# Attention with two kinds of heads and a gated feed-forward: the second chunk's keys and queries come as casting loads of a pair of heads in the software queue

## The chip, the cores and the metric

The kernel runs on one core of a Trainium2 chip. The metric is the device time of one execution in microseconds; the time of the kernel before is a median of three runs. "PE" in profile rows is TensorE, "PEld" its weight loads, "DVE" VectorE, "ACT" ScalarE, "POOL" GpSimd, "SP" SyncE. The "software queue" holds the DMAs that POOL issues (it can cast while loading), the "hardware queue" those that SP and ACT issue.

## What is computed

Four batches, eight heads, 768 positions, head size 64. Three heads see all earlier positions, five see a window of 64 and the first four positions. The attention output, 3072 tokens of 512, goes through a feed-forward of width 2048 with a gated activation.

```python
scores = scale * np.matmul(q, k.transpose(0, 1, 3, 2))       # q, k, v: (4, 8, 768, 64) f32
causal = rel >= 0
stream_keep = causal & (is_sink | in_win)                    # 4 sinks, window 64
a = np.exp(np.where(mask, scores, -1e9) - max)
out = np.matmul(a / a.sum(), v)                              # -> x: (3072, 512)
h = x @ w_in                                                 # (512, 2048)
g = h * (1.0 / (1.0 + np.exp(-beta * h)))
return g @ w_out                                             # (2048, 512)
```

## The kernel before

The work is cut into eight chunks of 384 tokens (three tiles of 128), two per batch. For each chunk the kernel brings keys and queries with the head dimension on partitions (two heads, a "pair", fill 128), makes scores in transposed form, exponentiates them on ScalarE, multiplies masks on VectorE, sums weighted values on TensorE (`products`, L882), scales (`x`, L906), transposes the result (`x_transposed`, L909), then runs the first product with `w_in` (L939, sixteen blocks of four matmuls), tanh on ScalarE (L941), the gate on VectorE (L943), the second product with `w_out` (L958), and stores 128 rows at a time. All data is computed in bf16 and summed in f32.

Every step is a `Task` with a planned duration; `Plan.run` (L128) plays the plan and so fixes, at build time, the order in which each engine's instructions stand. TensorE's next task is the one with the lowest key of `pe_key` (L1013): its place in the feed-forward (`STEPS`), moved by `LEAD`, `LEADS` and by a table `NUDGE` of single corrections. At run time each engine goes through its list in order and only waits on semaphores. Where TensorE would idle in the first 36 us by the plan, `fill` (L1036) puts matmuls on zeros.

The first two chunks start the kernel and get their own way of loading, from chunk three on rows are cast by the software queue and transposed by DMA on SP.

Chunks one and two (`F32_KQ`, L362, is true for chunk 0 and, by `F32_1 = "kq"`, for chunk 1): `load_pair` (L555) loads a pair's keys or queries as f32 from the hardware queue, 192 KB, one DMA; `keys_ramp` (L633) casts them to bf16 (`cast`, on VectorE or ScalarE, L458 by the helper `copy`), transposes them with three full 128 x 128 matmuls against the identity (L654), and copies the result from PSUM into `KT` or `QT` (L458). The token order inside a pair is p-major ("(p t) d"), so that each partition reads 768 bytes in one piece; the copy puts the columns back in order with a stride.

The software queue carries, in the order of `SW_ORDER` (L357), the values of chunk 0 (`v0`, three DMAs of 128 KB written), a hold (`h1`, a one-element POOL copy that waits for the first chunk's last key load and lets the second chunk's fourth pair start), the four column blocks of `w_in` (`i0` to `i3`, 512 KB each), the values of chunk 1 (`v1`) and the four row blocks of `w_out` (`o0` to `o3`). Not more than eight DMAs of this queue are in flight: an issue waits for the landing of the one eight places earlier.

`load_heads` (L602) and the branch of `keys_rows` (L662) for `KQ_PE` chunks are in the code but not used before the change.

```python
F32_1 = "kq"                                                       # L350
SW_ORDER = "v0 h1 i0 i1 v1 i2 o0 i3 o1 o3 o2".split()              # L357
casts[name] = P.add(f"cast{name}{c}.{p}", [dve(n, 0.53), act(n, 20)], [LD[name, c, p]], ...)   # L644
```

Of the kernel before, what the change touches and what calls it, by code (L numbers as in the profile page):

```python
# [9 lines left out]
BF16 = mybir.dt.bfloat16  # L10
# [68 lines left out]
class Plan:  # L79
# [10 lines left out]
    BEFORE, BEHIND, MARGIN, EARLY, LATER, FIRST = 1000.0, 1000.0, 100.0, 8900.0, 1000.0, 900.0  # L90
# [17 lines left out]
    def next_landing(self):  # L108

        now, left = self.moved, {q: [x[:] for x in l] for q, l in self.queues.items()}  # L110
        while True:
# [7 lines left out]
            turn = sum(left[q][0][2].land[2] for q in live)  # L119
# [120 lines left out]
    [(3, 3), (3, 2), (3, 3), (2, 2), (3, 3), (1, 1), (2, 2), (3, 3), (2, 2)],  # L240
    [(4, 3), (4, 3), (4, 0), (3, 0), (4, 3), (2, 3), (8, 8), (4, 4), (3, 3), (3, 3), (3, 3)],
    [(11, 10), (11, 11)],
    [(12, 12), (12, 11), (10, 10), (8, 0)],
    [(11, 10), (11, 11)],
    [(12, 12), (12, 12), (9, 7), (9, 2)],
    [(11, 10), (11, 11)],
    [(12, 12), (12, 12), (7, 7), (11, 2)],
]
F2_LAG = 12.0
RAMP = 40000.0  # L250
NUDGE = {
# [93 lines left out]
}  # L345
PARTS = [(3, 3)] * 4
LAST = 1
F32_1 = "kq"
MASK_C = 1
LEAD = 0.95  # L350
LEADS = {2: 1.6, 6: 0.9, 3: 0.9, 5: 0.9, 7: 1.0}
STORE_LATE = 1000.0
TURN = 33.0
X_PE = 3
PACE = {3: (2,), 5: (2, 8), 6: (3, 2), 7: (4, 0)}
FILL_END, FILL_SPARE = 36000.0, 120.0
# [18 lines left out]
def kernel(  # L375
# [13 lines left out]
    nc = tc.nc  # L389
# [709 lines left out]
```

## Time and profile before

| | |
|---|---|
| median of three runs | 225.69 us (224.97, 225.69, 227.6) |
| the profiled execution's own time | 225.52 us |
| its span, first to last instruction | 223.4 us, granted TensorE clock 0.998 |
| TensorE busy | 213.5 us (96%) |
| VectorE, ScalarE, POOL busy | 155.5, 144.5, 84.2 us |
| read from memory, written to it | 27.27 MB, 6.29 MB |
| first matmul of the first product, of the second chunk's | 22.12 us, 42.38 us |

The page of the profile has busy time by engine, then the span in 40 slices of 5.6 us with each engine's busy tenths, the DMA queues, the chain of waits that ended last, and the costliest groups of instructions. A timeline row gives start and length in us, engine, line, operation, output<-input tiles, and in brackets how long the engine sat idle ahead of it and what ended that. A matmul's row is longer than the time to the next one, since matmuls are pipelined; the time from start to start is what it costs.

### The profile page before, as it was taken

What the parts mean: (1) busy time and instruction counts of PE and PEld (TensorE: products, weight loads), DVE (VectorE), ACT (ScalarE), POOL (GpSimd) and SP (SyncE); (2) the same over time, 40 slices, a digit from 0 to 9 for tenths busy, and PEclk for the clock granted to TensorE, in tenths of its full rate; (3) what the DMA queues carried; (4) which work ended last, traced back from release to release, by engine and by line L of the source; (5) the groups of instructions that cost most, each with busy time, mean ns of one, the idle gap of its engine ahead of it and who ended that gap; (6) DMA issues with size and microseconds to landing.
All of it is one profiled execution on the core that took longest, in us unless ns stands there. A gap on an engine that the chain in (4) does not pass through costs nothing.

```text
span 223.4 us, 5079 instructions
## 1 busy us (share of the span) xinstructions
PE 213.5 (96%) x1842; PEld 123.7 (55%) x1866; DVE 155.5 (70%) x445; ACT 144.5 (65%) x292; POOL 84.2 (38%) x125
## 2 busy tenths in 40 slices
PE   7978999999999999999999999999999999999993
PEld 3546556554565555655554566455564655555552
DVE  5979995487687697779766777578765874437341
ACT  4887984484856798278756978069837793268310
POOL 7931533746995929800990397000000000000000
PEclk9999999999999999999999999999999999999999
DMA  6999999999999999998999499930104130011022
GB/s 197 247 238 197 201 206 199 123 149 144 167 151 135 210 160 179 142 130 226 86 136 166 128 143 154 137 111 22 47 18 102 47 85 2 0 50 47 1 94 94
DMA packets 102568, 28.32 MB, mean 127 GB/s; under 512 B 90880, under 2 KB 99600, under 8 KB 102544
## 3 DMA queue, kind: packets, MB, share of 16 engines
q0 software_dynamic: 67200, 12.07, 75.4%
q1 hardware_dynamic: 34480, 15.41, 33.2%
q10 hardware_dynamic: 864, 0.53, 0.8%
q8 instruction: 14, 0.23, 0.4%
q14 instruction: 10, 0.08, 0.1%
HBM read 27.27 MB, written 6.29 MB: 150 GB/s over the span
## 4 chain that ended last, share of the span: by engine, by line
PE 80%; DMA 10%; ACT 3%; DVE 3%; issue 2%; SPq 1%; ACTq 0%
PE bank L958 34%; PE bank L939 34%; PE bank L898 6%; PE bank L844 5%; DMA ks<-in_k_dram 5%; DMA xT<-x 2%; DMA qs<-in_q_dram 2%; SPq L560 1%; ACT th L941 1%; DVE gT L943 1%; ACT es L862 1%; PE bank L920 1%; DMA out_dram<-osb 1%; DVE VO L458 1%; DVE osb L971 0%
## 5 line engine op out<-in xcount | busy, mean ns | idle before, releaser
L941 ACT ACTIVATE th<-bank,beta_h 128x384 f32<-128x384 f32 x128 | 73.3, 590 | 36.6 <-PE bank L939 29.4
L939 PE MATMUL bank<-xT,w_in_sb 128*128 128x384 bf16 x512 | 90.5, 326 | 0.3 <-DMA xT<-x 0.2
L958 PE MATMUL bank<-w_out_sb,gT 128*128 128x512 bf16 (+1 forms) x376 | 87.7, 370 | 1.8 <-issue 0.6
L943 DVE SCALAR_TENSOR_TENSOR gT<-th,bank 128x384 bf16<-128x384 f32 x128 | 68.7, 550 | 26.4 <-ACT th L941 21.7
L862 ACT ACTIVATE es<-bank 128x512 bf16<-128x512 f32 (+3 forms) x137 | 62.8, 561 | 22.0 <-PE bank L844 18.0
L939 PEld LDWEIGHTS <-w_in_sb 128*128 128x128 bf16 x512 | 48.5, 98 | 34.0 <-issue 0.8
L958 PEld LDWEIGHTS <-gT 128*128 128x128 bf16 x400 | 37.5, 98 | 37.0 <-issue 0.5
L598 POOL DMA_DIRECT2D ks<-in_k_dram x36 | 26.9, 785 | 8.7 <-DMA w_out_sb<-in_moe_w_out_dram 3.1
L598 POOL DMA_DIRECT2D qs<-in_q_dram x36 | 26.9, 789 | 6.4 <-DMA w_out_sb<-in_moe_w_out_dram 3.6
L870 DVE TENSOR_TENSOR es<-es,M 128x384 bf16<-128x384 bf16 (+3 forms) x73 | 23.0, 333 | 6.7 <-ACT es L862 6.0
L570 POOL DMA_DIRECT2D VX<-in_v_dram x24 | 21.7, 946 | 0.0
L898 PEld LDWEIGHTS <-es 128*128 128x128 bf16 x472 | 17.2, 97 | 6.2 <-issue 2.3
L971 DVE TENSOR_SCALAR osb<-bank 128x512 f32<-128x512 f32 (+1 forms) x18 | 11.6, 646 | 11.7 <-PE bank L958 11.5
L844 PE MATMUL bank<-QT,KT 64*128 64x128 bf16 (+2 forms) x275 | 19.8, 242 | 0.0
L898 PE MATMUL bank<-VX,es 128*128 128x65 bf16 x392 | 17.9, 193 | 0.6 <-DVE x L906 0.6
L844 PEld LDWEIGHTS <-KT 64*128 64x128 bf16 x275 | 12.3, 94 | 9.9 <-issue 8.5
L906 DVE TENSOR_TENSOR x<-bank,rec 128x384 bf16<-128x384 f32 x32 | 17.0, 548 | 0.3
L870 DVE TENSOR_TENSOR es<-es,Mc 128x128 bf16<-128x128 bf16 (+1 forms) x42 | 9.9, 249 | 5.8 <-ACT es L862 5.5
L458 DVE COPY VO<-VX 128x512 bf16<-128x512 bf16 (+3 forms) x20 | 9.2, 475 | 2.1 <-DMA VX<-in_v_dram 2.0
L844 PE MATMUL bank<-QT,KO 64*128 64x128 bf16 x75 | 10.2, 217 | 0.0
L898 PE MATMUL bank<-VO,es 128*128 128x65 bf16 x80 | 9.1, 193 | 1.1 <-DVE VO L458 1.1
L969 ACT ACTIVATE osb<-bank 128x512 f32<-128x512 f32 (+1 forms) x9 | 4.7, 526 | 8.3 <-DVE osb L971 4.9
(58 smaller groups left out, 84.6 us busy)
## 6 DMA issues: line engine op xcount, KB each, us to landing
out_dram<-osb SPq DMA_DIRECT2D x23, 256.0 KB, 2.4
VX<-in_v_dram POOLq DMA_DIRECT2D x24, 128.0 KB, 6.9
ks<-in_k_dram POOLq DMA_DIRECT2D x36, 64.0 KB, 4.3
qs<-in_q_dram POOLq DMA_DIRECT2D x36, 64.0 KB, 4.4
w_in_sb<-in_moe_w_in_dram POOLq DMA_DIRECT2D x4, 512.0 KB, 15.9
w_out_sb<-in_moe_w_out_dram POOLq DMA_DIRECT2D x4, 512.0 KB, 16.1
ks<-in_k_dram SPq DMA_DIRECT2D x8, 192.0 KB, 4.7
qs<-in_q_dram SPq DMA_DIRECT2D x6, 192.0 KB, 6.4
```

Source lines behind the costliest of these rows:

```text
L570: LD["v", c, t] = dma(f"ldv{c}.{t}", "POOL", 800, 880, TURN, deps, lambda e, t=t, r=r: e.dma_start(out=VH[c].buf[:, t, :, 0:D], in_=v[b, : ...
L598: ROW[name, c, t] = [dma(f"row{name}{c}.{t}.{a}", "POOL", 750, 440, TURN, list(deps), lambda e, t=t, a=a, r=r, i=i, src=src: e.dma_start(o ...
L844: nc.tensor.matmul(bank.buf[:, at * 128:(at + n) * 128], x["k"](), QH[c].buf[half(a), x["p"], x["q"] * 128:(x["q"] + n) * 128], start=not ...
L862: te = P.add(f"exp{c}.{s}", [act(w * 128)], [t], c * 100 + first_p * 10, lambda _, w=w, bank=bank, es=es: nc.scalar.activation(out=es.buf[ ...
L870: nc.vector.tensor_mul(e, e, other)
L898: nc.tensor.matmul(view()[:, i, a, 0:D + 1], e.buf[:, at * 128:(at + 1) * 128], val(), start=(j == 0), stop=(j == len(lst) - 1))
L906: nc.vector.tensor_mul(xo, view()[:, :, :, 0:D], rec.buf[:, 0:nt].to_broadcast([128, nt, 2, D]))
L939: nc.tensor.matmul(bank.buf[:, 0:n], w_in_sb[:, mo, fi * 128:(fi + 1) * 128], XTH[c].buf[:, mo, 0:n], start=(mo == 0), stop=(mo == MO - 1))
L941: t = P.add(f"th{c}.{fi}", [act(n, 97)], [t, t_beta], c * 100, lambda _, fi=fi, bank=bank, th=th: nc.scalar.activation(out=th.buf[:, 0:n], ...
L943: GATE[c, fi] = P.add(f"gate{c}.{fi}", [dve(n)], [t], c * 100, lambda _, fi=fi, bank=bank, th=th: nc.vector.scalar_tensor_tensor(out=GH[c] ...
L958: nc.tensor.matmul(bank.buf[:, 0:hi - lo], GH[c].buf[:, fi, ns * 128:(ns + 1) * 128], w_out_sb[:, fi, lo:hi], start=(fi == 0), stop=(fi == ...
L971: nc.vector.tensor_scalar(out=osb.buf[:, l:h], in0=src, scalar1=0.5, scalar2=None, op0=ALU.mult)
```

## The change

With `F32_1 = ""` the second chunk's eight loads leave the hardware queue, and its casts and `keys_ramp` tasks go. `load_heads` is rewritten: one DMA of the software queue per pair and name brings a pair of heads as bf16, cast on the way, p-major as before (`pairs_of`), 96 KB written in pieces of 384 bytes. `keys_rows` transposes chunk 1 from there with 64-column matmuls, one per head and tile, each writing its half of the output partitions: six per pair and name where there were three. The copy out of PSUM keeps the stride. The hold `h1` is gone. `SW_ORDER` puts the pairs `p0 p1 p2` ahead of `i1`, and `p3` ahead of `v1`; the output blocks now stand behind all input blocks, in order.

The numbers that set the order are new as a whole: session sizes, `NUDGE` (most entries), `LEAD`, `LEADS`, `PACE`, `RAMP`, `TURN`, `FIRST`, and a factor `MIX` in the plan's share of the queues. They alter the build-time order only. `KQ1_AFTER` and the new branch of `landed` are not used, since no hold is left.

```diff
-    BEFORE, BEHIND, MARGIN, EARLY, LATER, FIRST = 1000.0, 1000.0, 100.0, 8900.0, 1000.0, 900.0
+    BEFORE, BEHIND, MARGIN, EARLY, LATER, FIRST, MIX = 1000.0, 1000.0, 100.0, 8900.0, 1000.0, 300.0, 1.25
...
-    [(3, 3), (3, 2), (3, 3), (2, 2), (3, 3), (1, 1), (2, 2), (3, 3), (2, 2)],
+    [(2, 3), (4, 2), (3, 3), (2, 2), (3, 3), (1, 2), (2, 1), (3, 3), (2, 2)],
...
 NUDGE = {
...
-F32_1 = "kq"
+F32_1 = ""
-LEAD = 0.95
-LEADS = {2: 1.6, 6: 0.9, 3: 0.9, 5: 0.9, 7: 1.0}
+LEAD = 1.65
+LEADS = {2: 1.8, 6: 0.9, 3: 0.9, 5: 0.9, 7: 0.9, 4: 0.8}
-PACE = {3: (2,), 5: (2, 8), 6: (3, 2), 7: (4, 0)}
+PACE = {3: (2,), 5: (2, 8), 6: (3, 10), 7: (4, 2)}
-SW_ORDER = "v0 h1 i0 i1 v1 i2 o0 i3 o1 o3 o2".split()
+SW_ORDER = "v0 i0 p0 p1 p2 i1 p3 v1 i2 i3 o0 o1 o2 o3".split()
...
+    def pairs_of(c, i):
+
+        return STG[c].buf[1][i].rearrange("p t g a d -> p (t g a d)").rearrange("p (g a x) -> p g a x", g=NP, a=2)
+
     def load_heads(g, key=None):
...
-            ROW[name, 1, g] = [dma(f"row{name}1.{g}.{a}", "POOL", 750, 330, TURN, [], lambda e, a=a, i=i, src=src: e.dma_start(
-                out=hold.buf[1][i][:, 0:nt, g, a, :], in_=src[b, a * NP + g, r, :].rearrange("(t p) d -> p t d", p=128)),
-                take=[hold], prio=10) for a in range(2)]
+            ROW[name, 1, g] = [dma(f"row{name}1.{g}", "POOL", 760, 800, 45, [], lambda e, i=i, src=src: e.dma_start(
+                out=pairs_of(1, i)[:, g], in_=src[b, :, r, :].rearrange("(a g) (p t) d -> p a g (t d)", a=2, t=nt)[:, :, g]),
+                take=[hold], prio=10)]
...
                         for t in range(nt):
-                            nc.tensor.transpose(tp[:, t, :], hold.buf[1][i][:, t, p].rearrange("p a d -> p (a d)"), ident)
+                            if c == 1:
+                                for a in range(2):
+                                    nc.tensor.transpose(tp[half(a), t, :], pairs_of(c, i)[:, p, a, t * D:(t + 1) * D], ident)
+                            else:
+                                nc.tensor.transpose(tp[:, t, :], hold.buf[1][i][:, t, p].rearrange("p a d -> p (a d)"), ident)
...
+                        if c == 1:
+                            tp, to = tp.rearrange("p (t j) -> p j t", t=nt), to.rearrange("p (j t) -> p j t", t=nt)
+                        copy(e, to, tp)
```

In POOL's list, which is the software queue, this stood behind the mask constants (`VX` are values, `ks_73` and `qs_74` the second chunk's keys and queries):

```order
L570 DMA VX_87<-in_v_dram 128x8x64 x3
L577 DMA w_in_sb<-in_moe_w_in_dram 128x4x512
L546 COPY ks_73<-ks_71 1x1
L577 DMA w_in_sb<-in_moe_w_in_dram 128x4x512
L570 DMA VX_88<-in_v_dram 128x8x64 x3
L577 DMA w_in_sb<-in_moe_w_in_dram 128x4x512
L583 DMA w_out_sb<-in_moe_w_out_dram 128x4x512
```

In the changed kernel the same place in POOL's list reads:

```order
L587 DMA VX_87<-in_v_dram 128x8x64 x3
L594 DMA w_in_sb<-in_moe_w_in_dram 128x4x512
L630 DMA ks_73<-in_k_dram 128x2x192
L630 DMA qs_74<-in_q_dram 128x2x192
L630 DMA ks_73<-in_k_dram 128x2x192
L630 DMA qs_74<-in_q_dram 128x2x192
L630 DMA ks_73<-in_k_dram 128x2x192
L630 DMA qs_74<-in_q_dram 128x2x192
L594 DMA w_in_sb<-in_moe_w_in_dram 128x4x512
L630 DMA ks_73<-in_k_dram 128x2x192
L630 DMA qs_74<-in_q_dram 128x2x192
L587 DMA VX_88<-in_v_dram 128x8x64 x3
```

The eight pair loads moved in, six ahead of the second weight block and two ahead of the second chunk's values; the copy that was the hold is gone.

In VectorE's list, around the copies of the first chunk's values (`VO`), the casts of the second chunk's keys and queries (`qkb<-ks_73`, `qkb<-qs_74`) stood so:

```order
L458 CAST qkb_76<-qs_74 128x2x3x64
L458 COPY KO_83<-KT_80 128x256
L458 COPY KO_83<-KT_79 128x3x4
L458 CAST qkb_77<-ks_73 128x2x3x64
L458 COPY VO_91<-VX_87 128x8x64
L458 COPY VO_92<-VX_87 128x8x64
L458 COPY VO_91<-VX_87 4x8x64
L458 COPY QT_86<-bank_66 128x384
L458 CAST qkb_77<-qs_74 128x2x3x64
L902 RECIPROCAL rec_138<-bank_64 128x6
L870 TENSOR_TENSOR es_114<-es_114,Mc 128x128
L906 TENSOR_TENSOR x_123<-bank_64,rec_138 128x3x2x64
```

Now VectorE's list has, at the copies of the first chunk's values:

```order
L473 CAST qkb_78<-qs_72 128x2x3x64
L473 COPY KO_83<-KT_79 128x128 x2
L473 COPY QT_85<-bank_65 128x384
L473 COPY VO_91<-VX_87 128x8x64
L473 COPY VO_92<-VX_87 128x8x64
L473 COPY VO_91<-VX_87 4x8x64
L931 RECIPROCAL rec_138<-bank_67 128x6
L935 TENSOR_TENSOR x_123<-bank_67,rec_138 128x3x2x64
L931 RECIPROCAL rec_139<-bank_64 128x6
L935 TENSOR_TENSOR x_123<-bank_64,rec_139 128x3x2x64
```

Only the first chunk's last cast stands ahead of the value copies; nothing of the second chunk stands between them and the scaling of the first chunk's output (`x_123`).

In ScalarE's list, up to the first tanh of the feed-forward (`th_130`), this stood before the change (`es` are exponentials, all of the second chunk here):

```order
L458 CAST qkb_78<-ks_73 128x2x3x64
L862 ACTIVATE es_119<-bank_67 128x256
L458 COPY xT_125<-bank_68 128x384
L458 COPY KT_80<-bank_69 128x384
L458 COPY KT_80<-bank_67 128x384
L458 COPY xT_125<-bank_64 128x384
L862 ACTIVATE es_120<-bank_70 128x384
L862 ACTIVATE es_94<-bank_67 128x384
L862 ACTIVATE es_110<-bank_63 128x384
L862 ACTIVATE es_121<-bank_66 128x512
L941 ACTIVATE th_130<-bank_64,beta_h 128x384
```

In the changed kernel ScalarE's list reads there:

```order
L473 COPY KT_80<-bank_67 128x384
L473 COPY QT_86<-bank_64 128x384
L891 ACTIVATE es_111<-bank_65 128x384
L891 ACTIVATE es_113<-bank_67 128x256
L891 ACTIVATE es_114<-bank_69 128x512
L891 ACTIVATE es_116<-bank_70 128x512
L970 ACTIVATE th_130<-bank_63,beta_h 128x384
L891 ACTIVATE es_112<-bank_66 128x512
L473 COPY QT_86<-bank_68 128x384
L473 COPY KT_80<-bank_67 128x384
L891 ACTIVATE es_115<-bank_64 128x512
L970 ACTIVATE th_131<-bank_69,beta_h 128x384
```

The first tanh moved ahead: four exponentials of the second chunk stand before it now, the other eighteen behind it, among the tanh.

More of the change, by code (lines that the diff above doesn't have):

```diff
@@ L118, in next_landing @@
                 continue
-            turn = sum(left[q][0][2].land[2] for q in live)
+            slow = {q: self.MIX if q != "POOL" and "POOL" in live and left[q][0][2].name[:2] == "ld" else 1.0 for q in live}
+            turn = sum(left[q][0][2].land[2] * slow[q] for q in live)
             part = {q: left[q][0][2].land[2] / turn for q in live}
@@ L538, in landed @@
             return (lambda: hold.buf[0][i][0:1, g, 0, 0:1]), [hold]
+        if kind == "v":
+            return (lambda: VH[key[1]].buf[0:1, key[2], 0, 0:1]), [VH[key[1]]]
         if kind == "wi":
@@ L561, in load_pair @@
             out=hold.buf[0][i].rearrange("p (a g) t d -> p a g (t d)", a=2)[:, :, g, 0:nt * D],
-            in_=src[b, :, r, :].rearrange("(a g) (p t) d -> p a g (t d)", a=2, t=nt)[:, :, g]), take=[hold], prio=prio, more=1500.0 if deps else 0.0)
+            in_=src[b, :, r, :].rearrange("(a g) (p t) d -> p a g (t d)", a=2, t=nt)[:, :, g]), take=[hold], prio=prio, more=2300.0 if deps else 0.0)
     def load_values(c, key=None):
@@ L675, in tr, with ev @@
                         for t in range(nt):
-                            nc.tensor.transpose(tp[:, t, :], hold.buf[1][i][:, t, p].rearrange("p a d -> p (a d)"), ident)
-                    t = P.add(f"T{name}{c}.{p}", [pe(n, nt)], ROW[name, c, p] if c == 1 else [x for t in range(nt) for x in ROW[name, c, t]], c * 100 + p * 10, tr, take=[bank], drop=[hold])
-                    made[c, p] = [P.add(f"E{name}{c}.{p}", [dve(n, 0.53), act(n)], [t], c * 100 + p, lambda e, p=p, bank=bank, holder=holder: copy(
-                        e, holder[c].buf[:, p, 0:n], bank.buf.bitcast(BF16)[:, 0:n]), take=[holder[c]], drop=[bank])]
+                            if c == 1:
[3 more added lines that the diff above has]
+                                nc.tensor.transpose(tp[:, t, :], hold.buf[1][i][:, t, p].rearrange("p a d -> p (a d)"), ident)
+                    t = P.add(f"T{name}{c}.{p}", [pe(2 * n, 2 * nt) if c == 1 else pe(n, nt)], ROW[name, c, p] if c == 1 else [x for t in range(nt) for x in ROW[name, c, t]], c * 100 + p * 10, tr, take=[bank], drop=[hold], mode=65 if c == 1 else 128)
+                    def ev(e, p=p, bank=bank, holder=holder):
+                        tp, to = bank.buf.bitcast(BF16)[:, 0:n], holder[c].buf[:, p, 0:n]
+                        if c == 1:
+                            tp, to = tp.rearrange("p (t j) -> p j t", t=nt), to.rearrange("p (j t) -> p j t", t=nt)
+                        copy(e, to, tp)
+                    made[c, p] = [P.add(f"E{name}{c}.{p}", [dve(n, 1.042 if c == 1 else 0.53), act(n)], [t], c * 100 + p, ev, take=[holder[c]], drop=[bank])]
                 continue
```

16 lines of the change are left out of this document (8 added, 8 removed), and 200 rows, old and new, of the table NUDGE.

## Prediction

> **What bounds the kernel now.** I read the page first, by engine and by slice.
>
> ```profile
> PE 213.5 (96%) x1842; PEld 123.7 (55%) x1866; DVE 155.5 (70%) x445; ACT 144.5 (65%) x292; POOL 84.2 (38%) x125
> PE   7978999999999999999999999999999999999993
> DVE  5979995487687697779766777578765874437341
> ACT  4887984484856798278756978069837793268310
> DMA  6999999999999999998999499930104130011022
> ```
>
> TensorE is full from the fifth slice (22 us) on; VectorE and ScalarE stand at 7 to 9 tenths in slices 2 to 6 and fall behind after that. The view by windows, cut at the first matmul of the first product (22.1) and at the second chunk's first one (42.4), says where time can still be found.
>
> ```profile
> 0.00:5.20 5.20, 3.90 (x13) 1.73 (x14) 2.71 (x16) 2.00 (x4) 4.05 (x18) 1.00 0.64 186
> 5.20:22.10 16.90, 14.32 (x200) 9.15 (x199) 14.55 (x48) 13.89 (x38) 8.72 (x12) 1.00 1.46 231
> 22.10:42.40 20.30, 19.82 (x199) 12.05 (x200) 16.16 (x45) 14.49 (x31) 8.48 (x12) 1.00 1.43 187
> 42.40:219.60 177.20, 175.23 (x1436) 100.75 (x1456) 121.75 (x338) 113.85 (x221) 63.00 (x85) 1.00 1.06 110
> ```
>
> After the length come PE, PEld, DVE, ACT and POOL busy, then clock, DMA and GB/s. From 42.4 on PE idles 2 us in 177: nothing to win, but a new order can lose. The clock is full. So the change must pay between 5 and 42 us. The timelines of VectorE, then TensorE, show that stretch.
>
> ```profile
> 15.44 0.36 DVE L458 CAST qkb<-ks 128x384 bf16<-128x384 f32 x1 [1.32 <-DMA ks<-in_k_dram]
> 15.71 0.87 DVE L458 COPY VO<-VX 128x512 bf16<-128x512 bf16 x3
> 17.46 0.36 DVE L458 CAST qkb<-qs 128x384 bf16<-128x384 f32 x1 [0.41 <-DMA qs<-in_q_dram]
> ```
>
> ```profile
> 15.45 0.45 PE L898 MATMUL bank<-VX,es 128*128 128x65 bf16 x9
> 16.64 0.19 PE L898 MATMUL bank<-VO,es 128*128 128x65 bf16 x1 [0.74 <-DVE VO L458]
> 19.63 0.50 PE L654 MATMUL bank<-idb,qkb 128*128 128x128 bf16 x6
> 19.96 0.33 PE L920 MATMUL bank<-idb,x 128*128 128x128 bf16 x3
> 22.12 3.41 PE L939 MATMUL bank<-xT,w_in_sb 128*128 128x384 bf16 x20
> 25.47 0.23 PE L844 MATMUL bank<-QT,KT 64*128 64x128 bf16 x2
> 25.54 0.22 PE L844 MATMUL bank<-QT,KO 64*128 64x128 bf16 x2
> 25.59 0.22 PE L844 MATMUL bank<-QT,KT 64*128 64x128 bf16 x2
> 42.38 5.85 PE L939 MATMUL bank<-xT,w_in_sb 128*128 128x384 bf16 x35
> ```
>
> VectorE sits in front of a cast of the second chunk's keys (1.32 us), and the copies of the first chunk's values queue behind it; the first weighted sum over values starts at 15.45, and the first product only at 22.12. The value loads themselves are late. POOL's own timeline tells landings, because each issue there waits for the load eight places earlier:
>
> ```profile
> 12.22 0.74 POOL L583 DMA_DIRECT2D w_out_sb<-in_moe_w_out_dram  x1 [0.65 <-DMA VX<-in_v_dram]
> 15.25 0.85 POOL L577 DMA_DIRECT2D w_in_sb<-in_moe_w_in_dram  x1 [2.28 <-DMA VX<-in_v_dram]
> 19.68 0.74 POOL L583 DMA_DIRECT2D w_out_sb<-in_moe_w_out_dram  x1 [3.59 <-DMA w_in_sb<-in_moe_w_in_dram]
> 22.80 1.58 POOL L583 DMA_DIRECT2D w_out_sb<-in_moe_w_out_dram  x2 [2.38 <-DMA w_in_sb<-in_moe_w_in_dram]
> 28.12 0.74 POOL L598 DMA_DIRECT2D ks<-in_k_dram  x1 [1.84 <-DVE es L870]
> 30.41 0.74 POOL L598 DMA_DIRECT2D ks<-in_k_dram  x1 [1.55 <-DMA w_out_sb<-in_moe_w_out_dram]
> 35.45 0.74 POOL L598 DMA_DIRECT2D ks<-in_k_dram  x1 [1.53 <-DMA w_out_sb<-in_moe_w_out_dram]
> 38.06 0.74 POOL L598 DMA_DIRECT2D qs<-in_q_dram  x1 [1.86 <-DMA w_out_sb<-in_moe_w_out_dram]
> ```
>
> So the third value load landed at about 15.0, the first weight block at 19.4, the second at 22.5. From 30.41 to 35.45 two more blocks land: 2.5 us for a block when only the software queue runs. From 22.80 to 28.12 three value loads and one block: 5.3 less 2.5, 0.9 us a value load. The hardware queue is the other half:
>
> ```profile
> qs<-in_q_dram SPq DMA_DIRECT2D x1, 192.0 KB, 3.7
> ```
>
> ```profile
> 8.55 10.89 DMA ks<-in_k_dram
> 40.81 1.73 PE bank L958 x8
> ```
>
> The first row is the first chunk's last pair load, issued at 4.2 (list of issues in that window): landed at 7.9. The second, from the chain of waits, is the second chunk's last key pair: landed at 19.4, so six further pairs and this one took 11.5 us in company with the values and weights, 1.6 us each.
>
> **First term: when the first product starts.** Away go eight SP loads, eight casts (seven on VectorE, one on ScalarE) and the POOL copy that held one of them back. The casts are worth 7 x 0.3 us of VectorE (0.36 busy, 0.27 to the next), 0.4 us of ScalarE, and the 1.7 us of waits shown. With the hardware queue empty after 7.9, three value loads at 0.9 can be in by 10.7 (9.9 if the first is then already there as the second chunk's loads let it be by 9.8; 12.6 if half of today's delay to 15.0 stays). ScalarE then sets the pace:
>
> ```profile
> 7.57 1.54 ACT L862 ACTIVATE es<-bank 128x384 bf16<-128x384 f32 x4
> 20.58 0.87 ACT L458 COPY KT<-bank 128x384 bf16<-128x384 bf16 x2
> 23.29 1.60 ACT L941 ACTIVATE th<-bank,beta_h 128x384 f32<-128x384 f32 x3
> ```
>
> By the new order 18 exponentials and one copy stand between 7.57 and the end of the first chunk's scores: 18 x 0.385 + 0.4 = 7.3, to 14.9; with 0.35 (rows overlap) 14.3. Weighted sum of the last pair, reciprocal, scaling, transpose and copy are 0.3 + 0.1 + 0.55 + 0.35 + 0.4, with hops about 2 us: 16.3 to 16.9. The same way took 7.1 us from the value landing before, which from 10.7 gives 17.8 and from 12.6 gives 19.7. I take 17.2 with ends 16.3 and 19.7.
>
> **Second term: the stretch to the second chunk's first product.** It took 20.26 us (22.12 to 42.38). By the order it gains: 30 transposes of 64 columns; 26 blocks of 128 score columns that used to run earlier; four matmuls of the second product; ten more changes between array shapes. A full transpose is 0.055 (six from 19.63 to 19.96), score matmuls on half the array start two at a time every 0.055, a matmul of the second product is 0.216 (1.73 for 8), and a first-product matmul 0.163 (5.85 less its tail, over 34), so twenty end at 25.37 and the change of shape to 25.47 costs 0.10. That is 26 x 0.028 + 4 x 0.216 + 10 x 0.10 = 2.6, plus the transposes: 30 x 0.055 = 1.65 if one follows the other, 0.83 if they run in pairs as the score halves do. That row is nearest, being half arrays too, so 0.83: 3.4, and 4.2 at the other end. The rest then holds four second-product matmuls fewer, -0.86.
>
> **Sum.** Start 17.2 - 22.1 = -4.9; stretch +3.4; rest -0.9: -2.4 on the profiled execution's own 225.52 (span 223.4 and 2.1 around it), which lies 0.2 under the median of 225.69. The time is 223.2. Ends: start 16.3 gives 222.3; start 19.7 with serial transposes gives 226.5.
>
> **What I cost at nothing.** The pair loads have no row. By bytes, 96 KB written, a weight block's rate (2.5 for 512 KB) gives 0.48 us, the value loads' (0.9 for 128 KB) 0.68, and the pair loads beside other traffic took 1.6. I take 0.6, nearest in queue and piece size. Then weight block one lands at 13.2, the six pairs at 16.8, block two at 19.3, the last pairs at 20.5, the next values at 23.2, block three at 25.7, all just ahead of their first user: walking the new order from 17.2 at the prices above, block two is due at about 20.4 and block three at 26.3. That cover is thin and is the second rival. In the software queue block two now stands behind six pair loads, the next values behind all eight, and the first output block behind the last input block, due only near 32. POOL issues eight more, 0.74 each, and its waits for the load eight places earlier stay, but by then the queue holds several loads of backlog. SP loses only issues; its transposes wait until 41 us as before. After 42 us the order is new, the count of score shape changes the same; the 2 us of idle there bound a gain, and I allow 1 us to either side, half of them.
>
> **A rule weighed.** The Trainium skill, "TensorEngine Tiling (Array Packing)", section "Key Properties", says that changing the tiling mode drains the array and that tiles work in parallel; the 0.10 and the paired rows agree, for halves by rows. The same page, "Restrictions and Gotchas", says that halves by columns, which these transposes use, cannot load weights fast. No run here shows that yet. By the first the sum is what I have; by the second it is the third rival.
>
> **The rivals.**
> *ScalarE becomes the bound, or the start moves less.* Beside the stretch the new order holds 22 exponentials, 16 tanh and 5 copies: 22 x 0.42 (the row's 0.385 and a tenth, ten being 512 wide) + 16 x 0.5 + 5 x 0.43 = 19.4 us, from about 16.5 to 36, when TensorE would reach the same tanh at about 35. One us later start or stretch: 224.2; two and a half: 225.6. Against it: VectorE loses its waits.
> *The pair loads are dear (slower than before).* Every us of eight pairs delays block three. At 0.95 each it lands at 28.5, 2.2 late, and the gain is gone; at 1.3 it lands at 31.3 and the time is 228.2. For it: 1.6 in mixed traffic. Against: there the hardware queue was the second party, and it is gone.
> *Weight loads of the transposes are not hidden.* The page's group for the scores' own weight loads shows a price:
>
> ```profile
> L844 PEld LDWEIGHTS <-KT 64*128 64x128 bf16 x275 | 12.3, 94 | 9.9 <-issue 8.5
> ```
>
> 30 x 0.094 is 2.8 instead of 0.83: 225.2. It is what the second statement of the Trainium skill's page would do here.
> *More than I count.* Start at 16.3 (222.3) and an order after 42 us that wins half of the 2 us of idle there: 221.3.
>
> **Chances.** Forecast (222.3 to 224.3 its own range) 0.42; ScalarE or late start 0.22; unhidden weight loads 0.05; dear loads 0.11; more than counted 0.20. About 1% (2.26 us, to 223.4) is what a measurement can tell from no change. Faster by over 1%: six tenths of the forecast's and all of the last, 0.45. Slower by over 1%: the dear loads, 0.11. Within: 0.44. The range leaves out most of the dear loads and the end of the lucky case: 220.9 to 226.2.
>
> **What would show it.** In the profile after: VectorE with no wait for a key cast and value copies near 11 to 12; the first product's first row near 17; the second chunk's first near 40.5; transposes of 64 columns starting two per 0.055; POOL's waits putting block two near 19. It is wrong if the first product starts after 19.5, if value copies still wait near 15, if first-product matmuls wait for weight loads between 20 and 30, or if TensorE idles over 3 us after 42.

## The result and the profile after

| | kernel before | changed kernel | predicted |
|---|---|---|---|
| median | 225.78 us (20 runs, 224.73 to 229.46) | 224.88 us (20 runs, 224.13 to 225.66) | 223.2 (220.9 to 226.2) |
| ratio | | 0.9946, 95% interval 0.9923 to 0.9969 | 0.989 |
| profiled execution, its span | 225.52, 223.4 us | 224.66, 222.9 us | |
| first product's first matmul | 22.12 us | 18.93 us | 17.2 |
| second chunk's first one | 42.38 us | 43.06 us | 40.5 (40.9 by its sum) |
| last matmul's start | 219.54 us | 218.76 us | 217.1 (by its sum) |

The kernel is about half a per cent faster, 0.9 us by the medians, where 2.4 were predicted. Ratios leave out executions that took over 1.5% longer than the fastest of their kernel, medians do not, so the two need not agree to the last digit. The difference of the profiled executions lies in these stretches: start -3.2, from there to the second chunk's first product +3.9 (20.26 to 24.13), the rest -1.5 (177.16 to 175.70), after the last matmul +0.3; together -0.45 us of span. The time around the span is 0.4 us shorter as well, and that is no chance: in all 42 executions of the changed kernel on record it is 1.72 to 1.92 us, in 126 of the kernel before 2.10 to 2.24. So some 0.4 of the 0.9 us do not come from the schedule inside the span; no run shows what they come from.

The view by windows of the changed kernel, cut at the same two matmuls (columns as before: length, busy us of PE, PEld, DVE, ACT, POOL):

```profile
0.00:5.50 5.50, 4.19 (x13) 1.78 (x14) 2.74 (x14) 2.00 (x3) 4.34 (x18) 1.00 0.64 188
5.50:18.90 13.40, 11.94 (x176) 7.56 (x174) 11.71 (x37) 9.85 (x27) 11.33 (x16) 1.00 1.53 202
18.90:43.10 24.20, 23.57 (x249) 13.96 (x251) 17.58 (x47) 19.00 (x42) 12.66 (x18) 1.00 1.50 182
43.10:218.80 175.70, 174.43 (x1438) 100.49 (x1454) 121.20 (x337) 113.22 (x221) 61.46 (x83) 1.00 1.10 108
```

The column to look at is ACT. Ahead of the first product ScalarE lost 4.0 us of work (13.89 to 9.85), and in the stretch behind it gained 4.5 (14.49 to 19.00). Much of it is exponentials of the second chunk: ten of the 22 used to run ahead of the first product, three do now. TensorE's timeline:

```profile
12.68 0.45 PE L927 MATMUL bank<-VX,es 128*128 128x65 bf16 x9
...
15.34 0.36 PE L699 MATMUL bank<-idb,ks 128*64 128x128 bf16 x6
...
17.35 0.34 PE L949 MATMUL bank<-idb,x 128*128 128x128 bf16 x3 [0.62 <-DVE x L935]
17.63 0.33 PE L873 MATMUL bank<-QT,KT 64*128 64x384 bf16 x1
...
18.93 0.82 PE L968 MATMUL bank<-xT,w_in_sb 128*128 128x384 bf16 x4
19.68 0.53 PE L699 MATMUL bank<-idb,qs 128*64 128x128 bf16 x12
20.04 0.33 PE L699 MATMUL bank<-idb,ks 128*64 128x128 bf16 x6
20.30 0.82 PE L968 MATMUL bank<-xT,w_in_sb 128*128 128x384 bf16 x4
...
28.12 0.28 PE L927 MATMUL bank<-VX,es 128*128 128x65 bf16 x4 [0.52 <-ACT es L891]
...
43.06 3.25 PE L968 MATMUL bank<-xT,w_in_sb 128*128 128x384 bf16 x19
```

The first weighted sum now starts at 12.68 (15.45 before) and no transpose waits for a cast of the second chunk. Eighteen transposes of 64 columns take 0.62 us (19.68 to 20.30), so they run two at a time. From there to 43.06 two waits are left (the views show waits from 0.15 us on): for the last scaling of the first chunk, and for ScalarE at 28.12. ScalarE's own timeline shows why:

```profile
14.11 1.56 ACT L891 ACTIVATE es<-bank 128x256 bf16<-128x256 f32 x4 [0.46 <-PE bank L879]
15.74 0.48 ACT L473 COPY KT<-bank 128x384 bf16<-128x384 bf16 x1
16.60 0.48 ACT L473 COPY QT<-bank 128x384 bf16<-128x384 bf16 x1 [0.39 <-DVE xT L473]
18.00 1.90 ACT L891 ACTIVATE es<-bank 128x384 bf16<-128x384 f32 x4 [0.91 <-PE bank L873]
19.79 0.58 ACT L970 ACTIVATE th<-bank,beta_h 128x384 f32<-128x384 f32 x1
...
36.33 0.61 ACT L970 ACTIVATE th<-bank,beta_h 128x384 f32<-128x384 f32 x1
37.71 0.58 ACT L970 ACTIVATE th<-bank,beta_h 128x384 f32<-128x384 f32 x1 [0.78 <-PE bank L968]
```

The first chunk's exponentials end at 15.67. After two copies ScalarE waits 0.91 us for the second chunk's first scores, and from 18.00 to 36.9 not one row has a wait. That unbroken run is new.

On the loads, POOL's timeline has one wait in this stretch:

```profile
14.39 0.70 POOL L630 DMA_DIRECT2D ks<-in_k_dram  x1 [2.07 <-DMA w_in_sb<-in_moe_w_in_dram]
```

It puts the first block of weights at about 14.1 (13.2 predicted). By issue and time to landing the third value load is in at 10.85 (10.7 predicted), and six pair loads follow the block from 14.64 to 17.28, 0.53 us each (0.6 predicted). The copies of the values, at 15.71 before, stand in VectorE's timeline at 11.27, with no wait:

```profile
11.27 1.17 DVE L473 COPY VO<-VX 128x512 bf16<-128x512 bf16 x3
```

### The profile page after: what moved, and what is told of

Same layout as the page of the kernel before. It is cut to its first block, busy times and chain, and to the rows that moved or that the text cites. A ratio compares the mean times of both kernels' runs of the same rounds, so it can differ in the third digit from the quotient of the medians.

```text
span 222.9 us, 5108 instructions
## 1 busy us (share of the span) xinstructions
PE 214.4 (96%) x1872; PEld 123.8 (56%) x1892; DVE 153.5 (69%) x435; ACT 144.3 (65%) x293; POOL 89.8 (40%) x132
## 3 DMA queue, kind: packets, MB, share of 16 engines
q0 software_dynamic: 69376, 12.85, 80.0%
## 4 chain that ended last, share of the span: by engine, by line
PE 91%; DVE 3%; ACT 2%; DMA 2%; issue 1%
PE bank L968 37%; PE bank L987 37%; PE bank L873 7%; PE bank L927 7%; DMA ks<-in_k_dram 2%; PE bank L949 1%; DVE qkb L473 1%; ACT es L891 1%; PE bank L699 1%; ACT th L970 0%; DVE KT L473 0%; DVE QT L473 0%; PE bank L861 0%; DVE M L518 0%; DVE x L935 0%
## 5 line engine op out<-in xcount | busy, mean ns | idle before, releaser
L891 ACT ACTIVATE es<-bank 128x512 bf16<-128x512 f32 (+3 forms) x137 | 63.8, 562 | 21.3 <-PE bank L873 20.3
L927 PE MATMUL bank<-VX,es 128*128 128x65 bf16 x392 | 18.6, 193 | 0.5 <-ACT es L891 0.5
L935 DVE TENSOR_TENSOR x<-bank,rec 128x384 bf16<-128x384 f32 x32 | 17.6, 552 | 0.4
L1087 POOL COPY ks<-gT 1x1 bf16<-1x1 bf16 x3 | 0.5, 177 | 27.1 <-DVE gT L972 27.1
L473 DVE COPY VO<-VX 128x512 bf16<-128x512 bf16 (+3 forms) x20 | 10.5, 541 | 0.1
L931 DVE RECIPROCAL rec<-bank 128x6 f32<-128x6 f32 x32 | 6.0, 189 | 5.9 <-PE bank L927 4.2
```

The source lines that it names most:

```text
L473: (nc.scalar.copy if e == "ACT" else eng[e].tensor_copy)(out=out, in_=in_)
L891: te = P.add(f"exp{c}.{s}", [act(w * 128)], [t], c * 100 + first_p * 10, lambda _, w=w, bank=bank, es=es: nc.scalar.activation(out=es.buf[ ...
L927: nc.tensor.matmul(view()[:, i, a, 0:D + 1], e.buf[:, at * 128:(at + 1) * 128], val(), start=(j == 0), stop=(j == len(lst) - 1))
L935: nc.vector.tensor_mul(xo, view()[:, :, :, 0:D], rec.buf[:, 0:nt].to_broadcast([128, nt, 2, D]))
```

## The experiments

Theory A was the prediction's own: the start of the first product carries the end, and it came late by the chain ahead of it. Theory B: TensorE's start is not what counts, since ScalarE and TensorE are both full behind it. From this grew theory S: the second chunk's first scores start ScalarE's run, and the run sets when the second chunk's product can begin.

The marks come from ScalarE's and TensorE's timelines of each profiled execution: first exponential; second chunk's first exponential; first product; second chunk's first product; start of the last matmul. Ratios are to the kernel before as it ran beside each (medians 225.5 to 226.0), with their 95% intervals; they compare better between rows than the medians do. The marks are of one execution each. The profiled execution of after_again took 445.45 us, twice the usual time, and has no marks here; one execution of all_three took 370.64. Why is not known.

The edits below are abridged. In them `F1` is the first product, `S` scores, `Tx` transposes of x, `Ex`, `Ek`, `Eq` copies out of PSUM, `KO` and `VO` small copies of keys and values; the number behind such a name is the chunk, from 0.

| kernel | median us | ratio | 1st exp. | 2nd chunk's exp. | 1st product | 2nd chunk's | last |
|---|---|---|---|---|---|---|---|
| before | 225.78 | | 7.57 | 14.46 | 22.12 | 42.38 | 219.54 |
| changed | 224.88 | 0.9946 (0.9923, 0.9969) | 8.04 | 18.00 | 18.93 | 43.06 | 218.76 |
| after_again | 224.95 | 0.9974 (0.9949, 0.9998) | | | | | |
| after_third | 224.70 | 0.9942 (0.9916, 0.9968) | 8.04 | 17.99 | 18.92 | 43.07 | 220.27 |
| path_alone | 225.84 | 1.0002 (0.9975, 1.0030) | 8.04 | 17.80 | 18.63 | 42.70 | 219.96 |
| order_alone | 226.80 | 1.0042 (1.0018, 1.0065) | 7.70 | 13.86 | 23.43 | 40.08 | 221.22 |
| twice_t | 224.83 | 0.9954 (0.9932, 0.9977) | 8.65 | 18.74 | 19.67 | 43.82 | 219.52 |
| scalar_more | 225.75 | 0.9998 (0.9973, 1.0023) | 8.63 | 18.28 | 19.21 | 44.26 | 219.96 |
| scalar_less | 224.57 | 0.9930 (0.9898, 0.9963) | 7.42 | 17.60 | 18.53 | 42.30 | 218.58 |
| f1_first | 226.06 | 1.0020 (0.9992, 1.0048) | 8.03 | 19.37 | 18.15 | 44.28 | 219.97 |
| scores_first | 225.06 | 0.9984 (0.9951, 1.0017) | 8.27 | 17.65 | 18.89 | 43.25 | 219.12 |
| list_swap | 224.76 | 0.9941 (0.9916, 0.9966) | 7.62 | 17.46 | 18.50 | 42.69 | 218.38 |
| pairs_first | 225.34 | 1.0002 (0.9976, 1.0029) | 7.76 | 18.09 | 19.02 | 43.16 | 218.85 |
| all_three | 224.66 | 0.9960 (0.9930, 0.9990) | 7.62 | 16.91 | 18.17 | 42.17 | 217.86 |
| mask_late | 224.78 | 0.9958 (0.9933, 0.9983) | 7.44 | 17.40 | 18.33 | 42.48 | 219.13 |
| all_four | 224.91 | 0.9969 (0.9939, 1.0000) | 7.94 | 17.57 | 18.83 | 42.83 | 218.75 |

**The two halves of the change.** The data path with the old tables, and the new tables with the old path:

```
path_alone:   SESSIONS, F2_LAG, RAMP, NUDGE, LEAD, LEADS, TURN, PACE, FIRST, MIX as before
order_alone:
-F32_1 = ""
+F32_1 = "kq"
-SW_ORDER = "v0 i0 p0 p1 p2 i1 p3 v1 i2 i3 o0 o1 o2 o3".split()
+SW_ORDER = "v0 h1 i0 i1 v1 i2 o0 i3 o1 o3 o2".split()
```

> The changed data path with the old numbers that set the order. Theory A (the time follows the start of the first product, and that is set by the chain of loads, casts, exponentials and values): the first product starts between 18 and 20 us and the kernel takes 0.99 to 1.00 of the kernel before. Theory B (TensorE and ScalarE are both full after the start, so an earlier start is given back): first product as early, but the second chunk's first one at 43 or later, and 1.00 to 1.01.

> The new numbers that set the order with the old data path (second chunk in the hardware queue with casts and full transposes, the old order of the software queue). Theory A: the first product stays at 21.5 us or later, 1.00 to 1.02 of the kernel before. Theory B, by which the rest after 43 us and not the start gave the gain: 0.993 to 0.997.

The path alone starts the first product 3.5 us earlier than the kernel before, at 18.63, and wins nothing (1.0002). Its view by windows:

```profile
0.00:18.60 18.60, 16.44 (x193) 9.20 (x193) 14.16 (x50) 12.04 (x30) 15.62 (x33) 1.00 1.27 197
18.60:42.70 24.10, 22.91 (x242) 13.47 (x243) 17.91 (x49) 18.36 (x41) 12.12 (x17) 1.00 1.49 182
42.70:220.00 177.30, 175.44 (x1436) 100.84 (x1456) 120.94 (x337) 114.44 (x222) 61.96 (x84) 1.00 1.12 109
```

The stretch grows by 3.8 us to 24.1, as long as the changed kernel's 24.2, though by the order it holds four matmuls fewer of the second product (24 for 28) and six transposes fewer: TensorE has 1.2 us of idle in it. Its two waits there are one for ScalarE and one for VectorE's copies of the second chunk's values:

```profile
20.77 0.36 PE L685 MATMUL bank<-idb,qs 128*64 128x128 bf16 x6 [0.42 <-ACT es L877]
28.85 0.19 PE L913 MATMUL bank<-VO,es 128*128 128x65 bf16 x1 [0.71 <-DVE VO L459]
```

The rest takes 177.3, as in the kernel before. So the early start was given back at once: the span is even 0.5 us longer than that of the kernel before beside it (median 224.1 for 223.6), and the shorter time around it (1.77 for 2.16) makes up for that. What the change wins inside the span comes from the new tables on the new path: four more matmuls (0.86 us) in a stretch that lasts 24 us anyhow, and a rest in which TensorE is idle 0.6 us less. Theory A's range reached up to 1.00 and so just holds the ratio; what falls is its mechanism, that the time follows the start. Theory B's other half falls too: the tables on the old path were to win 0.3 to 0.7% and cost 0.4%.

**What sets the stretch: TensorE or ScalarE.** Every transpose of 64 columns issued twice; two more exponentials on ScalarE; two copies from ScalarE to VectorE (`order` is the plan's list, "exp1" and so on belong to the second chunk):

```
twice_t:
+    for _ in range(2):
         for a in range(2):
             nc.tensor.transpose(tp[half(a), t, :], pairs_of(c, i)[:, p, a, ...], ident)
scalar_more:
+    for uid in ("exp1.5:1", "exp1.8:0"):       # behind each of these
+        nc.scalar.activation(out=scr, in_=zeros, func=ACTF.Exp, scale=scale)   # 128x512
scalar_less:
+    for uid in ("Eq1.2:0", "Ek1.2:0"):
+        order[at(uid)].engine = "DVE"
```

> Every transpose of 64 columns is issued twice. Theory A (TensorE is full between 19 and 43 us, and these transposes run two at a time): 30 more in that stretch at 0.027 us, 0.8 us, and up to 0.2 us before it, so 0.8 to 1.0 us over the changed kernel, about 0.998 of the kernel before. If their weight loads are not hidden, 30 at 0.094 us: 2.8 us more, 1.007. Theory B, by which ScalarE and not TensorE sets the stretch: under 0.4 us.

> ScalarE gets two more exponentials of 512 columns (0.48 us each) on zeros, between 22 and 26 us. If ScalarE sets the stretch, the second chunk's first weighted sum moves from 28.1 to 29.0 and the second chunk's first product and the end move by 0.8 to 1.0 us. If TensorE sets it, ScalarE's idle time after 37 us takes them up and the end moves by under 0.3 us.

> Two of the second chunk's copies out of PSUM (0.36 us each on ScalarE) go to VectorE at the same place of its list. If ScalarE sets the stretch, TensorE's wait of 0.52 us at 28.1 goes and the end comes 0.4 to 0.5 us earlier, 0.994. If not, no change within 0.1 us, or 0.3 us later where VectorE's copies of 0.55 us delay the next scores.

With thirty more transposes in it the stretch is 24.15 us, as long as without (24.13), and the median does not move. Added up from start to start, the stretch's transposes went from 1.21 to 2.05 us, 0.028 each, so they ran in pairs and their weight loads hid. TensorE had just the room for them: the wait of 0.52 us at 28.12 is gone in that run, and from the first product to the second chunk's first weighted sum it took 9.33 us for 9.20. (That execution is 0.7 us later throughout because its first exponential is 0.6 later, 8.65.) Two exponentials of 0.48 us more on ScalarE lengthen the stretch by 0.92 us and the time by 0.8 to 1.05. In TensorE's timeline of that run the waits for ScalarE multiply:

```profile
26.36 1.46 PE L968 MATMUL bank<-xT,w_in_sb 128*128 128x384 bf16 x8 [0.32 <-ACT es L891]
28.09 0.23 PE L873 MATMUL bank<-QT,KT 64*128 64x128 bf16 x2 [0.28 <-ACT QT L473]
29.44 0.28 PE L927 MATMUL bank<-VX,es 128*128 128x65 bf16 x4 [0.53 <-ACT es L891]
44.26 1.95 PE L968 MATMUL bank<-xT,w_in_sb 128*128 128x384 bf16 x11
```

With 0.7 us less on ScalarE the stretch is 0.36 us shorter and the wait at 28 falls to 0.28; the median is 0.1 to 0.4 lower, which its interval does not tell from the changed kernel's three. VectorE took those two copies over and did not lengthen the stretch.

So ScalarE sets the stretch, but only up to the second chunk's first weighted sum (28.12). From there to the second chunk's first product TensorE has 0.1 us of idle in each of these runs and takes 14.94 us in the changed kernel, 14.82 in twice_t and scalar_more, 14.89 in scalar_less: that part is TensorE's. All added work stood ahead of it; what more work behind 28 us would cost was not tried.

**Which start counts.** The first product ahead of the second chunk's scores, and the opposite:

```
f1_first (TensorE's list):
+    behind("F1.0.1:0", "Ex0.1:0")                    # first block of the first product
+    S1.3, S1.0, S1.1, S1.2 behind F1.0.1             # the second chunk's first scores
+    behind("Ek1.1:0", "Ex0.1:0")                     # VectorE: xT copies ahead of a key copy
scores_first:
+    ahead("KOs1.0:0", "x0.3:0")
+    S1.3, S1.0, S1.1 ahead of Tx0.3                  # the first chunk's last transposes
```

> In the changed kernel the first four matmuls of the first product are moved ahead of the second chunk's first four score blocks in TensorE's list, and its two xT copies ahead of a key copy in VectorE's. Theory S (ScalarE's unbroken run, which starts with the second chunk's first scores, sets when the second chunk's product can start): first product 0.6 to 0.8 us earlier, the second chunk's first exponential 1.0 to 1.3 us later than the changed kernel's 18.0, second chunk's first product 0.6 to 1.2 us later, and the end with it, 0.999 of the kernel before. Theory A (the start of the first product carries the end): 0.7 us less, 0.993.

> The opposite: three of the second chunk's score blocks go ahead of the first chunk's last transposes in TensorE's list, with a small key copy ahead of the last scaling in VectorE's. Theory S: second chunk's first exponential 0.5 to 0.7 us earlier, first product 0.2 to 0.4 us later, second chunk's first product and the end 0.3 to 0.6 us earlier, 0.993 to 0.994. Theory A: 0.3 us later, 0.997.

In TensorE's timeline of f1_first the first product stands here:

```profile
18.15 0.91 PE L968 MATMUL bank<-xT,w_in_sb 128*128 128x384 bf16 x4 [0.28 <-DVE xT L473]
```

and in ScalarE's the second chunk's first exponentials here:

```profile
19.37 0.76 ACT L891 ACTIVATE es<-bank 128x384 bf16<-128x384 f32 x2 [2.31 <-PE bank L873]
```

The first product starts 0.78 us earlier and the kernel is 1.1 to 1.4 us slower than the changed one: ScalarE waits 2.31 us, its run starts 1.37 us later, and the second chunk's product 1.22 us later. This is close to theory S (by its numbers 1.0 to 1.3, 0.6 to 1.2, and a ratio of 0.999 where 1.0020 was measured), and against A in sign. Among the kernels with ScalarE's list unchanged behind its run's start (changed, after_third, twice_t, list_swap, f1_first, pairs_first, mask_late) that product comes 24.9 to 25.2 us after the second chunk's first exponential, wherever the first product stands. The opposite move missed: that exponential came 0.58 us sooner after the first one, but with the same list on ScalarE the second chunk's product then came 25.6 us after it, in the main because the first tanh had to wait for the first product:

```profile
19.98 0.58 ACT L970 ACTIVATE th<-bank,beta_h 128x384 f32<-128x384 f32 x1 [0.41 <-PE bank L968]
```

The ratio is 0.9984 where 0.993 to 0.994 was expected. An earlier start of the run is worth nothing where the run then breaks.

**Ahead of the first product.** VectorE's list around the first chunk's last scaling; POOL's first value load held until the second key pair is cast; and a mask copy, first used at 18.9 us, moved from 5.1 to behind the value copies:

```
list_swap:
+    x0.3 ahead of KO1.0; KOs1.0 behind Ex0.3; KO1.1 behind Ex0.1
+    order[at("Ek1.1:0")].engine = "ACT"
hold_values (ahead of the first load of values, on POOL):
+    nc.gpsimd.tensor_copy(out=VH[0].buf[0:1, 0, 0, 0:1], in_=<cast of key pair 1>[0:1, ...])
mask_late:
+    behind("masks:8", "VOs0:0")
```

> In the changed kernel the last scaling of the first chunk's output and its copies after the transposes are moved ahead of the second chunk's copies in VectorE's list, and one key copy goes to ScalarE, which stood idle there. Theory A (the start is late because the second chunk's work stands in the lists, and the end follows the start one to one): TensorE's 0.62 us wait for x shrinks to 0.2, first product at 18.5, second chunk's at 42.6, 0.4 us less, 0.994 where the changed kernel has 0.996. Theory B (ScalarE's run of exponentials and tanh sets the stretch, whatever the start): the same time within 0.1 us unless the second chunk's first exponential moves too.

> POOL's first value load waits for the cast of the second key pair, so that POOL writes no descriptors while VectorE makes its first casts and masks. Theory A (the first exponential stands at 8.0 us because those casts and copies take 0.76 in place of 0.3 us beside POOL's issues): the first exponential near 7.2, the values 1.5 us later, the first product 0.3 to 0.8 us earlier. Rival (the late landings of the hardware queue set the first exponential, the values' landing the rest): the first exponential at 7.9 to 8.1, the first product 0.5 to 1.0 us later, and the end with it.

> In the changed kernel one copy of VectorE that makes a mask first used at 18.9 us is moved from ahead of the second key pair's cast to behind the first chunk's value copies, where VectorE stood idle for 0.9 us. If VectorE beside POOL's issues sets the first exponential, and the end follows it: the second key cast ends 0.25 to 0.7 us earlier, first exponential at 7.3 to 7.8, time 0.3 to 0.5 us under the changed kernel's, 0.994. If the landings of the loads set it: no change within 0.1 us.

The swap did nothing by itself: from the last weighted sum of the first chunk to the first product it took 2.84 us, and 2.85 in the changed kernel; the small copies had stood in gaps. The 0.4 to 0.5 us by which its marks up to 43 us are earlier are mostly the first exponential's (7.62 for 8.04). The kernel that holds the loads back can't be judged by its time: ten of its twelve executions had a mean granted clock of 0.98 and took 228.5 to 230.7 us, the two at 1.0 took 225.92 and 226.04, about as the kernel before; the ratio of 1.0091 (1.0046 to 1.0136) mixes the two. Why the clock was lower is not known. Of its profiled execution, at 0.983, only the first 20 us are read. VectorE's rows, first of the changed kernel, then of hold_values:

```profile
4.22 0.79 DVE L473 CAST qkb<-ks 128x384 bf16<-128x384 f32 x1 [1.65 <-DMA ks<-in_k_dram]
5.09 0.76 DVE L518 COPY M<-M 128x512 bf16<-128x512 bf16 x1
6.03 0.76 DVE L473 CAST qkb<-ks 128x384 bf16<-128x384 f32 x1
```

```profile
4.33 0.36 DVE L473 CAST qkb<-ks 128x384 bf16<-128x384 f32 x1 [1.77 <-DMA ks<-in_k_dram]
4.77 0.28 DVE L518 COPY M<-M 128x512 bf16<-128x512 bf16 x1
5.46 0.36 DVE L473 CAST qkb<-ks 128x384 bf16<-128x384 f32 x1
18.87 0.36 DVE L473 COPY xT<-bank 128x384 bf16<-128x384 bf16 x1 [2.18 <-PE bank L949]
```

While POOL issued nothing, casts and copies took less than half as long, and the first exponential stood at 7.67 (8.04 in the changed kernel; 7.2 was expected). But every later load moved with the first, the pairs were issued 2.8 us later (10.13 for 7.32), and their transposes stand in TensorE's list ahead of the first chunk's last transposes:

```profile
18.03 0.36 PE L699 MATMUL bank<-idb,ks 128*64 128x128 bf16 x6 [2.28 <-DMA ks<-in_k_dram]
```

So the first chunk waited too (2.18 us at 18.87 on VectorE): the thin cover of the prediction's second rival, seen from the other side. With the mask copy moved, VectorE's second key cast stood at

```profile
5.33 0.76 DVE L473 CAST qkb<-ks 128x384 bf16<-128x384 f32 x1
```

and the first exponential at 7.44. But the first cast of that execution had been a quick one (0.36 us), and in six others with a quick first cast and the mask copy at its old place the second stood at 5.38 to 5.46, and in four of them the first exponential at 7.42 to 7.76. So the move gained 0.1 us at the cast, and the median is the changed kernel's beside it (224.78, 224.70). Quick or slow changes with the landing of the first keys, by chance as far as the lists go: of sixteen profiled executions eleven had a quick first cast (hold_values among them), with the first exponential at 7.42 to 7.94 but for two (8.27, 8.63), and five a slow one, with 8.03 to 8.65. Both of the changed kernel's were slow, the kernel before's was quick.

The rest has chance of its own. Between 80 and 120 us another profiled execution of the changed kernel (after_third) has waits that its first has not, and ends 1.5 us later (last matmul 220.27 for 218.76); from its view of waits there:

```profile
DVE VO L473 <- DMA VX<-in_v_dram: 1.9, 2, 1.6
PEld L968 <- issue: 1.1, 3, 0.5
```

**Together.** The first pair's loads ahead of the first block of `w_in`; then scores_first, scalar_less and this one; then with the mask:

> The changed kernel once more, as the measure for the others. Both theories expect 0.992 to 0.997 of the kernel before, the first product at 18.9 us and VectorE's copies beside POOL's issues slower by up to 0.45 us, though not always the same ones; if its first exponential again stands near 8.0 us and not near 7.6, the late start is the order's and not chance.

> The first pair's two loads go ahead of the first input block in the software queue; the engines' lists stay. The pair then lands near 12.0 in place of 15.2, the block near 15.2 in place of 14.1, 3.7 us ahead of its user. If the start waits for the pair in the executions whose exponentials come early (a wait of 0.9 us stood there at 14.1 in one of them), the time falls by 0.2 to 0.5 us; if not, it stays within 0.1 us.

> The earlier scores, the two copies from ScalarE on VectorE, and the first pair ahead of the first block, together. Theory S: 0.4 and 0.35 us off the stretch and up to 0.2 off the start, 223.9 us, 0.991 to 0.992 of the kernel before. Theory A: 0.1 us less than the changed kernel at most, 0.996.

> The changed kernel once more beside the next two. 0.994 to 0.998 of the kernel before. Where its first cast starts by 4.18 us it takes 0.36 and the first exponential comes before 7.8; where it starts at 4.20 or later it takes 0.74 to 0.80 and the first exponential comes at 8.0 or later.

> The same together with the earlier scores, the two copies moved from ScalarE to VectorE, and the first pair ahead of the first input block. First exponential as in the run with the mask alone, second chunk's first exponential at 16.5 to 17.0, its first product at 41.6 to 42.2, 223.9 to 224.3 us, 0.990 to 0.993 of the kernel before. If the landings set the start: 0.995 to 0.996 as without the moved mask.

Loading the pair first did not help. The two combinations, of which theory S expected 223.9 and 223.9 to 224.3 us, reach the second chunk's product 34.55 and 34.89 us after their first exponential, for 35.02 in the changed kernel, so at most 0.5 us is theirs, and their medians (224.66, 224.91) are not told from the changed kernel's three (224.70 to 224.95). No version was shown to beat it.

## Why the prediction was right in sign and wrong in size

Of the 2.4 us that were forecast the span won 0.45. The start is short by 1.7 us, the stretch by 0.5, the time after the last matmul by 0.3; the rest gives 0.6 back. With the measured start in it the prediction's own sum would have been -0.7.

**First term (the start): failed, by 1.7 us.** The casts, their waits and the late values went as said; values, pairs and blocks landed within 0.1 to 0.9 us of their forecasts, all of them later. The step that failed is "ScalarE then sets the pace": 18 exponentials and one copy from 7.57 to 14.9, and the way from there to the first product "with hops about 2 us". Measured: the first exponential at 8.04 (0.47, which goes with the slow first cast), the run 7.6 for 7.3 us with two waits for scores (0.3), and from its end to the first product 3.26 us for 2.3 (0.95). Of the last, f1_first shows 0.78 to be work of the second chunk that stands ahead of the first product: its first scores in TensorE's list, a key copy in VectorE's.

**That an earlier start carries to the end: failed as well, and this is the deeper fault.** path_alone wins 3.5 us at the start and nothing at the end, and f1_first starts earlier and ends later. While the old kernel's first product was still to come, ScalarE made ten of the second chunk's 22 exponentials. Taking the waits away moved 4.5 us of ScalarE's work behind the start.

**Second term (the stretch): 3.4 predicted, 3.9 measured, in part for the wrong reason.** The prices were right where they could be read (transposes in pairs at 0.028 us). But up to 28 us the stretch is not their sum on TensorE: thirty more transposes did not lengthen it, 0.96 us of ScalarE cost 0.92.

**The rest: -0.9 predicted, -1.5 measured,** within the 1 us allowed. With the new tables on the new path it never took less than 175.7 us and took that in seven executions; with the old ones, on either path, it took 177.2 and 177.3, of which 0.9 are the four matmuls. The time around the span, taken as 2.1 us before and after, fell to 1.8; the prediction put that at nothing.

**The rivals.** ScalarE as the bound, or a late start (0.22, 224.2 to 225.6), is what happened, and both halves of it did. Its working had the run at 19.4 us from 16.5 to 36; it lasted 18.9, from 18.0 to 36.9. That the time lies where it put it is in part luck: 2.2 us of later start and longer stretch alone would give 225.4, and a rest and a time around the span that were both shorter than forecast took some 0.7 us off, net of the 0.3 behind the last matmul. It deserved the larger chance: the order's rows on ScalarE, quoted ahead of the prediction, show 18 exponentials of the second chunk among the tanh, and TensorE's first weighted sum of that chunk waits for them ten microseconds after the run's start. Dear pair loads did not come (0.53 us each), nor unhidden weight loads: at the prediction's 0.094 us they would have cost 2.8 us once, and as much again in twice_t. The weight loads of these transposes took 0.11 us each, no time of their own. The Trainium skill's "TensorEngine Tiling (Array Packing)", section "Restrictions and Gotchas", excludes fast weight loads for halves by columns. The trace does not speak against that, a load of all 128 columns took 0.10 us here, but it cost no time.

**Slips in the working,** without weight for the outcome: half of the delay of the third value load ends at 12.85 us, not 12.6. The 5.3 us to 28.12 were read as landings, but that row waits for VectorE; value loads landed about every 0.85 us in the changed kernel, where 0.9 was taken. The sum puts the second chunk's product at 40.9, not 40.5.

**Open:** how much of the other 0.6 us in the rest is the new order's, since waits for transfers of up to 1.6 us come and go there in one and the same kernel, and no run took those away; and what shortened the time around the span.

## What to carry to other kernels

A wait that is removed is worth only what the other engines did not do in it: before counting an earlier start as time won, add up, engine by engine, the work that used to be done during the wait and now stands behind it. The marker to forecast is the start of the longest unbroken run, here ScalarE's, as long as the run stays unbroken, and not the start of the engine that is busiest over the whole span. To find which engine sets a stretch, add half a microsecond of harmless work to each in turn: one of them passes it on in full. The answer holds for the place where the work was put: here ScalarE set the stretch up to 28 us, and behind that TensorE had next to no idle time left.

## What the runs showed of the hardware

VectorE's copies and casts within SBUF stand still for a while beside POOL's DMA issues: the first cast of 128x384 took 0.36 us where it started by 4.18 us and 0.74 to 0.80 where it started at 4.20 or later with POOL issuing (hold_values, with POOL quiet, 0.36 at 4.33); a copy of 128x512 took 0.27 or 0.76. Where the first cast was quick with POOL issuing, the next instruction was not (128x384, 0.62 to 0.68 us for 0.24). The copies of keys and queries out of PSUM took 0.54 to 0.56 either way. The Trainium skill's "SBUF — State Buffer", section "SBUF: two separate sides", has VectorE and GpSimd share one pair of ports under an exclusive lock, and names VectorE's two-port modes as what contends; the rows agree in kind, with 0.3 to 0.5 us lost each time, less than one issue takes (0.7 to 1.2 us). With a landing of the keys a tenth of a microsecond later the first exponential came some 0.4 us later (middle of the eleven 7.67, of the five 8.04), and the marks up to 43 us with it; that the cast alone does this is not shown, since two of the quick ones are late too.
